# Seven products of quarters for eight in the FFN of a routed-attention kernel

## The chip, the cores and the metric

The kernel runs on one core of a Trainium2 chip. The metric is the device time of one execution in microseconds (us); a time of the kernel is the median of several runs. A profile shows one execution: its span goes from the first to the last recorded instruction, and its own time is a little longer than the span.

## The reference

Two blocks in float32. The first is attention with pooled queries: 8 batches, 8 heads, 1,152 keys of 64 dimensions; two neighbouring queries are averaged, which leaves 576 query rows.

```python
q_pool = q.reshape(B, H, S // 2, 2, D).mean(axis=3)
scores = scale * np.matmul(q_pool, k.transpose(0, 1, 3, 2))
attn = np.exp(scores - max); attn = attn / (attn.sum(axis=-1, keepdims=True) + 1e-9)
x = np.matmul(attn, v)                  # joined over the heads: (8, 576, 512)
```

The second picks, in each batch, the 128 tokens with the highest gate score, and adds a gated feed-forward network (FFN) to them alone; the other tokens pass unchanged.

```python
scores = np.einsum('bsd,d->bs', x, w_gate)
top = np.argpartition(-scores[b], 128)[:128]
h = np.maximum(x[b, top] @ w1, 0.0)     # 512 -> 1024
out[b, top] = x[b, top] + sigmoid(scores[b, top])[:, None] * (h @ w2)   # 1024 -> 512
```

## The kernel before, in words

The work goes pair by pair: a pair is two heads of one batch, 4 pairs a batch, 32 in all. A pair's 576 queries are done in two halves of 288, so the main loop in `run` has 64 halves, plus one turn at the end. The order of all instructions is written out by hand; each engine works through its own queue in that order, and semaphores hold an instruction until what it reads or overwrites is ready.

One turn h of the loop emits, among other things, the following.

- On odd h, the DMAs on SP's queue: `load_pair` (keys `kb`, queries `qb`) two pairs ahead, `load_values` (`v_sb`), and `stored`, which writes a finished pair's `x` to the output (L964).
- `scores` (L807): 36 matmuls on PE in 9 groups. Each group takes one of four PSUM tiles from `banks` (two banks each), and ACT turns it into exponents `p` (L825). PE may run four tiles ahead of ACT.
- `folded` (L850): POOL adds thirds of `p` into `acc` (L857, three instructions), DVE reduces `p` and `acc` into `fold` (L862), which gives the sums of the softmax.
- `multiplied` (L919): POOL makes `prod` from the half two turns earlier and the gate weights; `gated` (L973): DVE reduces it into `red`.
- On even h, `prepare_pair` (L726): POOL adds neighbouring queries (`qp`), and DVE transposes `kT` and `qT` for the pair whose scores begin two turns later.
- `weighted` (L827): 36 matmuls on PE for the half before, then ACT's copy `two` (L844) and POOL's add `av` (L846); `drained`: DVE's transpose `avb` (L915).
- On odd h, `normalized` (L932): DVE's reciprocal `rec`, POOL's product `x` (L956).
- `units`: each batch that is being routed is moved on by one step, newest batch first.

`routed` (L997) is the route of one batch, a generator that is cut into steps by `yield`. A step ends at a `yield` of something true. The steps of a batch, one a turn, begin when its last pair is done: gate scores gathered (`groups`, `line`, `total`) and sent through DRAM to a row `sc_row`; ranks by comparison, on DVE, with two or three of five tiles a step (L1082, L1091, L1101); ranks sent through DRAM (`row_rank`, `lines`); the chosen tokens found on DVE (`pick`, L1161), POOL's `index` (L1170) and the gather of the 128 rows by an indirect DMA on POOL's queue (`xe`, L1178); PE's transposes into `xeT` (L1192); layer 1 (L1203, 32 matmuls of 128 columns in two PSUM tiles, and ACT's Relu, L1211); layer 2 (L1216, 8 matmuls of 512 columns), ACT's product with the gate (`y`, L1235), POOL's add to `xe` (L1238) and an indirect DMA that writes the rows back (L1239). So a batch has one turn with a burst of layer 1 and the next with a burst of layer 2.

The last three batches differ. Layer 2 of batch 5 is held back until after the loop. There, `run` (L1371 on) interleaves by hand the rest of batch 5 (`older`), the FFN of batch 6 (`old`) and the whole route of batch 7 (`new`): `diag` (L1043), its broadcast by matmul (L1053), columns (L679), ranks, `meta` (L1147), the gather, the FFN. Work of `older` and `old` fills PE while `new` waits.

`tile_pool`s give the buffers: a name in a pool has `bufs` slots, and a new tile of that name waits until the readers of the slot's last tile are done.

## Time and profile before

| | before |
|---|---|
| median of 3 runs | 707.98 us (707.88 to 709.09) |
| the profiled execution's own time | 707.99 us |
| its span | 706.3 us |
| mean granted TensorE clock | 0.999 |
| PE, weight load, DVE, ACT, POOL busy | 695.8, 499.9, 494.4, 442.8, 484.9 us |
| L1203 (layer 1), PE busy | 59.3 us in all |
| L1216 (layer 2), PE busy | 57.3 us in all |
| data moved by DMA | 82.86 MB, mean 117 GB/s |

Engines are named PE (matmul), PEld (weight load), DVE, ACT, POOL and SP, and L1203 is a line of the kernel. A group's row has its busy time, the mean length of one instruction, and the idle time of the engine ahead of it with what ended it. The chain that ended last is followed back from the last instruction, at each step to what released it. Each float32 matmul is recorded as two instructions, so counts of PE are twice those of the code.

### The profile page before, as it was taken

What the parts mean: (1) busy time and instruction counts of PE and PEld (TensorE: products, weight loads), DVE (VectorE), ACT (ScalarE), POOL (GpSimd) and SP (SyncE); (2) the same over time, 40 slices, a digit from 0 to 9 for tenths busy, and PEclk for the clock granted to TensorE, in tenths of its full rate; (3) what the DMA queues carried; (4) which work ended last, traced back from release to release, by engine and by line L of the source; (5) the groups of instructions that cost most, each with busy time, mean ns of one, the idle gap of its engine ahead of it and who ended that gap; (6) DMA issues with size and microseconds to landing.
All of it is one profiled execution on the core that took longest, in us unless ns stands there. A gap on an engine that the chain in (4) does not pass through costs nothing.

```text
span 706.3 us, 23391 instructions
## 1 busy us (share of the span) xinstructions
PE 695.8 (99%) x9948; PEld 499.9 (71%) x9948; DVE 494.4 (70%) x793; ACT 442.8 (63%) x963; POOL 484.9 (69%) x452
## 2 busy tenths in 40 slices
PE   8999999999999999999999999999999999999996
PEld 5668889977857678577775777767776677767573
DVE  3877777896549965499654987549784597869540
ACT  6677777777547774477745777467754777577210
POOL 5877777877668685586955879557884777866520
PEclk9999999999999999999999999999999999999999
DMA  9888887849692296825867258652877428442200
GB/s 181 172 170 181 182 166 139 151 95 164 116 169 57 66 165 126 154 52 106 166 104 135 52 126 159 119 106 52 163 127 134 86 53 172 72 82 60 47 31 35
DMA packets 389490, 82.86 MB, mean 117 GB/s; under 512 B 376640, under 2 KB 376640, under 8 KB 389376
## 3 DMA queue, kind: packets, MB, share of 16 engines
q1 hardware_dynamic: 387872, 76.49, 57.4%
q0 software_dynamic: 1280, 4.20, 1.7%
q8 instruction: 80, 1.31, 0.8%
q10 hardware_dynamic: 224, 0.59, 0.3%
q14 instruction: 34, 0.28, 0.1%
HBM read 69.65 MB, written 11.59 MB: 115 GB/s over the span
## 4 chain that ended last, share of the span: by engine, by line
PE 92%; POOL 3%; issue 1%; DVE 1%; DMA 1%; ACT 1%; SPq 0%; POOLq 0%; DVEq 0%; ACTq 0%
PE ps L818 38%; PE ps L836 37%; PE ps L1203 8%; PE ps L1216 7%; POOL acc L857 2%; DMA kb<-in_k_dram 1%; PE ps L1192 1%; POOL prod L925 0%; ACT p L825 0%; POOL x L956 0%; DVE fold L862 0%; POOL av L846 0%; SPq L759 0%; PE ps L1147 0%; PE ps L1053 0%
## 5 line engine op out<-in xcount | busy, mean ns | idle before, releaser
L825 ACT ACTIVATE p<-ps 128x576 f32<-128x576 f32 x576 | 319.2, 691 | 2.6 <-PE ps L818 2.3
L857 POOL TENSOR_TENSOR acc<-p 128x576 f32<-128x576 f32 x192 | 266.1, 1413 | 50.4 <-ACT p L825 50.0
L818 PE MATMUL ps<-qT,kT 64*64 64x288 f32 x4608 | 296.0, 405 | 0.3 <-ACT p L825 0.3
L836 PE MATMUL ps<-p,v_sb 64*64 64x288 f32 x4608 | 294.1, 403 | 0.0
L836 PEld LDWEIGHTS ps<-p,v_sb 64*64 64x64 f32 x4608 | 213.2, 133 | 67.8 <-ACT p L825 14.3
L818 PEld LDWEIGHTS ps<-qT,kT 64*64 64x64 f32 x4608 | 193.3, 132 | 89.8 <-ACT p L825 18.5
L862 DVE TRANSPOSE_TENSOR_REDUCE fold<-p 128x54 f32<-128x1728 f32 x64 | 126.0, 1969 | 117.2 <-ACT p L825 117.2
L862 DVE TRANSPOSE_TENSOR_REDUCE fold<-acc 128x54 f32<-128x1728 f32 x64 | 124.8, 1951 | 42.0 <-POOL acc L857 41.9
L844 ACT COPY two<-ps 128x576 f32<-128x576 f32 x64 | 40.9, 638 | 126.1 <-PE ps L836 113.2
L846 POOL TENSOR_TENSOR av<-two 128x288 f32<-128x288 f32 x64 | 51.1, 798 | 28.9 <-ACT two L844 27.3
L956 POOL TENSOR_TENSOR x<-avb,rec 128x576 f32<-128x576 f32 x32 | 37.0, 1157 | 43.1 <-DVE rec L954 27.1
L1203 PEld LDWEIGHTS ps<-xeT,w 128*128 128x128 f32 x512 | 57.8, 192 | 2.7 <-issue 2.6
L1203 PE MATMUL ps<-xeT,w 128*128 128x128 f32 x512 | 59.3, 277 | 0.0
L1216 PE MATMUL ps<-w,hT 128*128 128x512 f32 x128 | 57.3, 598 | 0.0
L925 POOL TENSOR_TENSOR prod<-avb,w_gate 128x288 f32<-128x288 f32 x64 | 51.3, 802 | 0.6 <-DVE avb L915 0.6
L902 ACT ACTIVATE sums<-total,tiny 32x18 f32<-32x18 f32 x124 | 38.2, 308 | 13.1 <-DVE total L893 11.4
L732 POOL TENSOR_TENSOR qp<-qb 128x576 f32<-128x576 f32 x31 | 43.8, 1412 | 2.5 <-DMA qb<-in_q_dram 2.5
L1216 PEld LDWEIGHTS ps<-w,hT 128*128 128x128 f32 x128 | 23.6, 190 | 28.1 <-issue 28.0
L735 DVE STREAM_TRANSPOSE kT<-kb 128x1152 f32<-128x1152 f32 x31 | 42.5, 1369 | 0.0
L1211 ACT ACTIVATE hT<-ps 128x512 f32<-128x512 f32 x16 | 9.6, 597 | 47.7 <-PE ps L1203 47.7
L1238 POOL TENSOR_TENSOR xe<-y,xe 128x512 f32<-128x512 f32 x7 | 8.9, 1270 | 38.3 <-ACT y L1235 38.3
L915 DVE STREAM_TRANSPOSE avb<-av 128x288 f32<-128x288 f32 x64 | 29.2, 456 | 7.2 <-POOL av L846 7.2
(95 smaller groups left out, 326.1 us busy)
## 6 DMA issues: line engine op xcount, KB each, us to landing
kb<-in_k_dram SPq DMA_DIRECT2D x124, 144.0 KB, 3.6
qb<-in_q_dram SPq DMA_DIRECT2D x124, 144.0 KB, 3.9
v_sb<-in_v_dram SPq DMA_DIRECT2D x124, 144.0 KB, 3.4
out_dram<-x SPq DMA_DIRECT2D x128, 72.0 KB, 3.0
lines<-row_rank SPq DMA_DIRECT2D x7, 640.0 KB, 4.1
w<-in_moe_w_dram SPq DMA_DIRECT2D x8, 512.0 KB, 4.8
sc_row<-row SPq DMA_DIRECT2D x7, 288.0 KB, 3.4
acc<-in_q_dram ACTq DMA_DIRECT2D x2, 288.0 KB, 4.2
```

The costliest lines, as they stand in the source:

```text
L732: nc.gpsimd.tensor_tensor(out=qp[:, :, :], in0=pair["q"][:, :, 0, :], in1=pair["q"][:, :, 1, :], op=ALU.add)
L735: nc.vector.transpose(kT.rearrange("p (c g i) -> p c g i", c=self.NC, i=BLK), pair["k"].rearrange("p (g c) d -> p c g d", c=self.NC),)
L818: nc.tensor.matmul(sc[keys, j, 0:n], lhsT=pair["kT"][rows, c * P + keys.start : c * P + keys.stop], rhs=pair["qT"][rows, qs], start=True, ...
L825: nc.scalar.activation(p[:, c // G, c % G, :, :], sc[:, :, 0:n], AF.Exp, scale=self.scale)
L836: nc.tensor.matmul(av[j * self.D : (j + 1) * self.D, e, 0:n], lhsT=half["pair"]["v"][keys, j, c, :], rhs=half["p"][keys, c // G, c % G, j, :],
L844: nc.scalar.copy(two[:, :, :], av[:, :, 0:n])
L846: nc.gpsimd.tensor_tensor(out=half["av"][:, :], in0=two[:, 0, :], in1=two[:, 1, :], op=ALU.add)
L857: nc.gpsimd.tensor_tensor(out=acc[:, u, :], in0=units[:, 0, u, :], in1=units[:, 1, u, :], op=ALU.add)
L862: nc.vector.tensor_reduce(fold[:, a, :], of.rearrange("p u (m d) -> p (u m) d", d=BLK), AX.X, ALU.add, apply_transpose=True,)
L925: self.nc.gpsimd.tensor_tensor(out=pair["prod"][:, ns, :], in0=pair["avb"][:, ns, :], in1=self.w_gate[:, hp : hp + 1, :].broadcast_to([P, ...
L1203: nc.tensor.matmul(pv[:, f, 0:w], lhsT=self.w1[:, c, (f0 + f) * P : (f0 + f + 1) * P], rhs=xeT[:, c, 0:w], start=(c == 0), stop=(c == self ...
L1216: nc.tensor.matmul(ps[0:w, 0 : self.Dm], lhsT=hT[:, f, 0:w], rhs=self.w2[:, f, :], start=(f == 0), stop=(f == self.NFC - 1),)
```

## The change

The FFNs of batches 0 and 1, 2 and 3, 4 and 5 are done together. The two batches' 2 x 128 tokens form one matrix, cut into quarters (a batch by half of the inner dimension), and the weights are cut into quarters as well. Each layer is then the product of two 2 x 2 block matrices, formed with seven block products in place of eight (Winograd's form). It needs four sums of input quarters (`input_sums`, on POOL), four sums of weight quarters (`weight_sums`, on DVE) and seven additions of products (`add`, on DVE, out of PSUM; the first product is copied by ACT).

- The weight sums of both layers are formed once, at the head of odd turns from h = 11 on, and kept in DRAM. One tile `tw` (128 x 4 x 1024) holds those of one layer; `load_sums` brings them back in four DMAs of 512 KB on SP's queue, a piece a turn.
- An even batch of the six stops after its transposes. The odd one goes on for both: input sums; a turn later layer 1 in one burst, and Relu, now from SBUF over 1,024 columns for each batch; a turn later the input sums of the hidden layer; four turns of loads; layer 2 in one burst; then, a turn each, add and write-back of the two batches; then four turns of loads.
- For batches 4 and 5, the held back step is layer 2 of both.
- Batches 6 and 7 keep the old form, which moves into a function `layers`.
- Buffers: `kb`, `qb`, `two`, `prod`, `sc_row` have one slot in place of two, `v_sb` two in place of three, `fold` and `groups` two in place of four; several scratch tiles share the slot of `pick`, and `diag` that of `lines`; `xe`, `index`, `own_gate` get more slots. The first pair is loaded into a `p` tile. V values are loaded one pair ahead rather than two, behind the keys and queries of the pair after.
- In the tail the pieces are counted anew.

In the built program, each two batches have 56 matmuls of 128 columns and 28 of 256 where there were 64 of 128 and 16 of 512.

```diff
+    def weight_sums(self):
+        for layer in (2, 1):
+            b11, b12, b21, b22 = (self.quarter(layer, i, j) for i in range(2) for j in range(2))
+            t1, t2, t3, t4 = (self.summed(layer, i) for i in range(4))
...
+            for i, (to, x, y) in enumerate(((t1, b12, b11), (t2, b22, t1), (t3, b22, b12), (t4, b21, t2))):
+                nc.vector.tensor_tensor(out=to, in0=x, in1=y, op=ALU.subtract)
+                nc.sync.dma_start(kept[:, i, :], self.tw[:, i, :])
+                yield
+
+    def load_sums(self, layer):
+        for i in range(4):
+            self.nc.sync.dma_start(self.tw[:, i, :], self.tw_kept[layer][:, i, :])
+            yield
...
-        kb = self.load.tile([P, self.KB, BLK], F32, name="kb")
-        qb = self.load.tile([P, self.QB, 2, BLK], F32, name="qb")
+        kb = self.load.tile([P, self.KB, BLK], F32, name="kb", bufs=1)
+        qb = self.load.tile([P, self.QB, 2, BLK], F32, name="qb", bufs=1)
...
-        v_sb = pair["v"] = self.load.tile([P, 2, self.NC, self.D], F32, name="v_sb", bufs=3)
+        v_sb = pair["v"] = self.load.tile([P, 2, self.NC, self.D], F32, name="v_sb", bufs=2)
...
-        two = self.small.tile([P, 2, n], F32, name="two", bufs=2)
+        two = self.small.tile([P, 2, n], F32, name="two", bufs=1)
...
+            if b >= self.paired:
+                yield from self.layers(token)
+            elif b % 2 == 0:
+                self.first_of_two = token
             else:
+                yield from self.layers_of_two([self.first_of_two, token])
...
+    def input_sums(self, a11, a12, a21, a22):
...
+        for to, x, y, op in (
+            (s1, a21, a22, ALU.add),
+            (s2, s1, a11, ALU.subtract),
+            (s3, a11, a21, ALU.subtract),
+            (s4, a12, s2, ALU.subtract),
+        ):
+            self.nc.gpsimd.tensor_tensor(out=to, in0=x, in1=y, op=op)
...
+    def seven_products(self, layer, a, s, c, shape):
...
+        tile = self.banks()
+        nc.scalar.copy(c11, product(bank(tile, 0), a11, b11))
+        yield False
+        add(u, product(bank(tile, 1), s2, t2), c11)
+        yield False
+        tile = self.banks()
+        p5 = product(bank(tile, 0), s1, t1)
+        add(c12, p5, u)
+        yield False
+        add(c21, product(bank(tile, 1), s3, t3), u)
+        add(c22, p5, c21)
+        yield False
+        tile = self.banks()
+        add(c11, product(bank(tile, 0), a12, b21), c11)
+        yield False
+        add(c12, product(bank(tile, 1), s4, b22), c12)
+        yield False
+        tile = self.banks()
+        add(c21, product(bank(tile, 0), a22, t4), c21)
+
+    def layers_of_two(self, tokens):
...
+        s = self.input_sums(*a)
+        yield True
...
+        yield from self.seven_products(
+            1, a, s, c, lambda bank: bank.rearrange("p (f n) -> p f n", n=P)[:, :, 0:w]
+        )
+        for tile in hidden:
+            nc.scalar.activation(tile[:, :, 0:w], tile[:, :, 0:w], AF.Relu)
+        yield True
+        s = self.input_sums(*c)
+        for i, _ in enumerate(self.load_sums(2)):
+            yield "hidden" if i == 3 else True
...
+        yield from self.seven_products(
+            2, c, s, [y[0:w, i * half : (i + 1) * half] for y in ys for i in range(2)],
+            lambda bank: bank[0:w, 0:half],
+        )
+        for token, y in zip(tokens, ys):
+            nc.scalar.activation(y[0:w, :], y[0:w, :], AF.Copy, scale=token["gate"][0:w, 0:1])
+        yield True
+        for token, y in zip(tokens, ys):
+            xe = token["xe"]
+            nc.gpsimd.tensor_tensor(out=xe[0:w, :], in0=y[0:w, :], in1=xe[0:w, :], op=ALU.add)
+            self.written(token)
+            yield True
+        if tokens[1]["b"] + 1 < self.paired:
+            for _ in self.load_sums(1):
+                yield True
...
                     if n + 2 < len(pairs):
                         loaded = self.load_pair(*pairs[n + 2])
-                        self.load_values(loaded)
+                    if n + 1 < len(pairs):
+                        self.load_values(upcoming)
...
+                if h > 10 and s == 1:
+                    next(sums, None)
...
-        pieces(older, self.NFC - 2)
+        pieces(older, 3)
         pieces(new, 1)
-        pieces(older, 2)
+        pieces(older, 1)
         pieces(new, 3)
         pieces(older)
-        pieces(old, self.NFC)
+        pieces(old, self.NFC // 2 - 1)
         pieces(new, 1)
         low = self.counted()
-        pieces(old, self.NFC - 3)
+        pieces(old, self.NFC // 2 + 1)
         pieces(new, 2)
         pieces(old)
```

## The prediction

> **What bounds the kernel.** I read the page's busy shares first, then the chain that ended last, in order of time, then each engine's timeline around one FFN and over the last 100 us.

> The first view is parts 1 and 4 of the page:

> ```profile
> PE 695.8 (99%) x9948; PEld 499.9 (71%) x9948; DVE 494.4 (70%) x793; ACT 442.8 (63%) x963; POOL 484.9 (69%) x452
> ...
> PE 92%; POOL 3%; issue 1%; DVE 1%; DMA 1%; ACT 1%; SPq 0%; POOLq 0%; DVEq 0%; ACTq 0%
> ```

> PE is never idle for long and is 92% of the chain; every microsecond of matmul taken out is won, unless another engine then comes last. The 3% of POOL is the place to watch. The chain in order of time around one FFN (start, length, what):

> ```profile
> 181.89 7.34 PE ps L1203 x64
> 189.23 4.53 PE ps L818 x72
> 193.76 4.37 PE ps L836 x72
> 198.12 7.06 PE ps L1216 x16
> 205.19 4.53 PE ps L818 x72
> ```

> A half (scores, then weighted) is 4.37 + 4.37 = 8.74 us where no FFN stands; each fp32 matmul is recorded as two passes. Layer 1 is 32 matmuls in 7.34 us (0.229 each), layer 2 is 8 in 7.06 us (0.883 each). The scores behind each burst take 4.53, so a burst costs 0.16 more. The same view of the tail:

> ```profile
> 640.39 1.16 POOL x L956
> 641.55 0.08 issue
> 641.63 0.23 POOL gate L1113
> 641.87 4.10 POOL acc L857 x3
> 645.97 0.76 POOL prod L925
> 646.73 0.76 POOL av L846
> 647.49 2.37 issue
> 649.90 0.93 POOL index L1170
> 650.83 0.27 issue
> 651.10 1.11 POOL xe L1178
> 652.25 2.66 POOL acc L857 x2
> ```

> Here, in the last halves, it is POOL's queue that runs end to end and leads to L1043's diag at 664.90; PE has no slack over it.

> **Removed: matmuls.** The built program has, per two batches, 56 matmuls of 128 columns and 28 of 256, for 64 of 128 and 16 of 512. Layer 1: 56 x 0.229 = 12.85 for 14.68. For 256 columns, the line through 114.7 ns (128) and 441 ns (512) a pass gives 223.6 ns, 0.447 a matmul: 28 x 0.447 = 12.52 for 14.12. Bounds for that product: 0.442 (half of 0.883) to 0.459 (twice 0.229), 0.4 us in all. Three pairs: 5.5 + 4.8 = **-10.3**. The 11 bursts in the loop, 0.16 each, go too: **-1.8**.

> **Added on POOL: the input sums.** Each pair gets four adds of 256 columns and four of 512. Rows: prod, 288 columns, 0.80; xe<-y,xe, 512 columns, 1.27. So 2.8 and 4.9 us per pair, 23 us over the run. In the sum this is nothing as such (POOL is 69% busy); it counts where POOL is the chain.

> In the tail it is. The sums of batches 4 and 5's hidden layer stand, in the built order, behind gate L1113 and ahead of the next half's acc, just where the lines above have 641.87. In the trace x ends there 5.2 us behind the half's start at 636.35; behind a burst, as it will stand after, it ends 3.5 behind (217.6 for the half at 214.09 in POOL's timeline). 4.9 - 1.7 = 3.2. The gather of batch 6 (651.10) is then later by that, and PE, which in the trace already waits 0.62 us for it at L1192, waits on. **+3.3**, between 0 (POOL catches up) and 4.9.

> **Added on DVE and ACT: the joins.** Seven DVE adds a layer, out of PSUM, 512 and 256 columns, and one ACT copy. The trace has adds of 384 columns at 0.554 and 576 at 0.758: 0.69 and 0.42, back to back some 0.62 and 0.36. ACT's Relu now comes after them, over 1,024 columns (about 1.0 us from L1211's 0.60 for 512), ahead of the next half's exponents in ACT's queue; behind those wait all scores. The trace prices such a late start: after the transposes at 171.86, the exponents start 1.41 us behind the scores and PE loses 0.70; after L1203 they start 0.80 behind and it loses 0.16. So PE loses the delay less 0.70.
> - Layer 1, first two pairs: POOL ends x 5.0 us into the half before (186.9 for 181.89), the sums at 7.9, acc 4.15 later, 3.4 into the half; then on DVE fold, 1.95, and sum, kT, qT, avb and total, another 3.3: the adds start about 8.7 us into the burst, keep up from the fifth product on and end 0.75 behind it, Relu 1.0 more: delay 1.75, loss 1.05 each, 2.1.
> - Third pair: the ranks of batch 6 (631.48 to 635.7 in DVE's timeline, about 3 us) stand ahead of the adds. They start near 11.7, end 3.2 behind the burst, exponents 4.15 behind: 3.45.
> - Layer 2 in the loop, two pairs: POOL's 4.9 us in the half behind layer 1 carries on, since DVE is full with ranks there (fold waits only 0.84 us for acc at 240.97). About 4.4 us are left when the picks are due. In the trace the rec behind a gather ends 256.2, 7.1 behind the end of weighted at 249.07; with 4.4 more the adds start 11.5 us into a 12.5 us burst and end 1.5 behind it, y 0.8 more: delay 2.3, loss 1.6 each, 3.2.
> Together **+8.75**. Bounds: 0.16 a burst if both engines are there in time (0.8), 14 if each burst waits as the third does, less the overlap of the layer 2 adds.

> The eight weight sums are one DVE add of 1,024 columns each at the head of odd halves; nearest rows are 0.758 (576 columns) and 1.37 (kT, 1,152). Steady halves have 1.5 to 2.5 us of DVE idle that hide it, but where ranks stand it does not: in the half of the transposes qT is ready at 265.9, 2.0 us ahead of the scores that need it (267.86), and two sums ahead of it make 2.5 less what POOL's waits absorb. Half a microsecond at each of the two batches of the first pair: **+1.0**, 0 to 3. [...]

> **Tail: two scatters, then a gather.** The rows on POOL and the landings over the tail's DMA view:

> ```profile
> 672.12 1.09 POOL L1239 DMA_INDIRECT out_dram<-xe,index  x1 [0.29 <-POOL xe L1238]
> 678.35 1.05 POOL L1178 DMA_INDIRECT xe<-out_dram,index  x1 [5.14 <-ACT own_gate L1155]
> ...
> out_dram<-xe,index POOLq DMA_INDIRECT x3, 2.9
> xe<-out_dram,index POOLq DMA_INDIRECT x1, 3.3
> ```

> Before, batch 5's write was long landed when batch 7's index came. After, layer 2 of batches 4 and 5 ends in the tail; its last three adds stand on DVE behind batch 7's ranks and pick (676.4 in the trace, about 676.9 after). From there: adds and y to 678.4, xe add 1.27, write of batch 4 at 680.0, landed 682.9; write of batch 5, which by the built program's semaphores waits for that landing, 683.0 to 685.9; the gather waits for the second landing, 686.0 + 3.3, so PE has batch 7's tokens at 689.4. PE meanwhile has 5.4 us of older's products, 2.75 of layer 1 of batch 6, 1.33 of meta and 4.59 of layer 1, and is out of work at 683.3. **+6.0**; 5.8 with the shortest landings seen (2.8), 8.1 with the medians over the run (3.4 and 4.4), 3 as a floor, if ranks and adds end 3 us sooner than their rows say.
> [...]

> **Hidden.** 28 more DMAs of 512 KB, on SP: the DMA view shows 4.8 us to land for such a piece of w, and the 16 engines are 60% busy. K and Q tiles are single now: the load waits for kT's read (243.25 to 244.6), then some 7 us of issue and 4 of landing, and the next kT read is 17.5 later. V is loaded behind it, needed 17 us after. Each costs nothing while 4 us of that are left. One buffer for two: its reader av is done at 243.84, the next write is due at 249.19, so 5.35 us of cover for POOL's lag of 4.9; gone, ACT's exponents wait, by the price above. prod's single tile is written at 240.91, 3.4 us behind the read it must await; fold, groups, sc_row and the tiles now shared with pick are reused in orders that already hold on DVE. The first pair's V values come behind the second load now: about 33 for a reader at 35.4.

> **Sum.** -10.3 - 1.8 + 3.3 + 8.75 + 1.0 + 6.0 = +6.95. Layer 2 of batch 4 moves from the loop to the tail; PE is full in both, so the move itself costs nothing, and its saving is in the 10.3. The profiled execution took 707.99 (span 706.3 and 1.7 around it), the median of the runs is 707.98. Forecast **715.0**.

> **Rivals.**
> - **The queues keep up (faster).** POOL and DVE work off the sums inside the bursts: adds reached before 8 us into each burst, batch 6's gather on time. Then the losses are 0.8 for the bursts, 0 for the sums, 6.0 in the tail: -12.1 + 6.8 = 702.7. For: both are at 70%, and L862 waits 117 us in total for ACT. Against: those waits lie in halves without ranks.
> - **Single buffers decide (slower).** If 11 us from kT's read to landed Q become over 17.5 because 28 pieces and the lines broadcasts share the engines, every pair stalls. For: the first ten slices show 80 to 90% DMA. At 0.4 us over 25 pairs, 10 on top: 725.
> - **Not done as said.** The built order has exactly 7 products a layer; with eight, the joins would leave 725. Next to nothing.

> **Chances.** Forecast and its neighbourhood (709.5 to 721) 0.60; queues keep up 0.15; a mix within 0.2% of before, about what a measurement here can tell from no change, 0.08; single buffers or worse 0.17. Faster 0.15, same 0.08, slower 0.77. Adding all low ends gives 700, all high ends 726; the range 704 to 722 leaves out half of the first rival and most of the last.

> **What would show it.** Right: two groups of matmuls at 12.85 and 12.5 us; scores behind the third layer 1 burst near 8 us; PE waiting about 4 us and 6 us at the last two transposes, for DMA; POOL and DVE near 73% each. Wrong: scores behind the bursts at 4.5, no wait of PE for a gather, or K loads as what ends PE's idle time.

## The result and the profile after

The changed kernel takes 780.75 us (median of 4 runs, 778.46 to 786.32) where the kernel before takes 707.94: a ratio of 1.104, 95% interval 1.098 to 1.110. Forecast were 715.0 in a range of 704 to 722. The sign was right, the size not: +73 us for +7.

The profiled execution took 781.66 us with a span of 779.9, 73.6 more than before. PE's busy time and idle time split that: busy 695.8 to 710.7 (+14.9), idle 10.5 to 69.2 (+58.7), though the change takes some 10 us of matmuls out. Parts 1 and 4 of the page after:

```profile
PE 710.7 (91%) x9972; PEld 543.9 (70%) x9972; DVE 530.8 (68%) x843; ACT 444.5 (57%) x963; POOL 511.4 (66%) x476
...
PE 58%; POOL 18%; issue 10%; DVE 6%; DMA 4%; ACT 3%; SPq 1%; POOLq 0%; DVEq 0%; ACTq 0%
```

No engine became the bound; PE's share of the chain fell from 92% to 58%, and what came in is waiting on others. (DVE and POOL at 68 and 66% of a longer span are lower than the 73% that the prediction wanted to see.) Where PE waits is read off its timeline. Here is the first burst of layer 1, start, length, what, and in brackets the idle time ahead with what ended it:

```profile
271.63 2.05 PE L1332 MATMUL ps<-xeT,w 128*128 128x128 f32 x16
274.45 3.81 PE L1332 MATMUL ps<-s,tw 128*128 128x128 f32 x32 [0.77 <-ACT hT L1344]
281.54 3.35 PE L1332 MATMUL ps<-s,tw 128*128 128x128 f32 x16 [3.28 <-DVE hT L1338]
284.68 2.30 PE L1332 MATMUL ps<-xeT,w 128*128 128x128 f32 x16
287.85 2.02 PE L1332 MATMUL ps<-s,w 128*128 128x128 f32 x16 [0.88 <-DVE hT L1338]
```

A product is 16 recorded matmuls. Products 2, 4 and 6 wait, 1, 3, 5 and 7 do not. The even ones go to the second bank of a PSUM tile whose first bank holds the odd product, and in the built program their first matmul waits on the engine that reads the odd one: ACT's copy for product 2, DVE's adds for 4 and 6. So PE does not run through a burst with the joins behind it; it stops in the middle until the joins have caught up. DVE's timeline at the same place shows why they are late:

```profile
275.08 1.98 DVE L895 TRANSPOSE_TENSOR_REDUCE fold<-acc 128x54 f32<-128x1728 f32 x1 [4.39 <-POOL acc L890]
...
279.93 0.67 DVE L1338 TENSOR_TENSOR y<-ps,hT 128x512 f32<-128x512 f32 x1
280.70 0.69 DVE L1338 TENSOR_TENSOR hT<-ps,y 128x512 f32<-128x512 f32 x1
284.92 0.69 DVE L1338 TENSOR_TENSOR hT<-ps,y 128x512 f32<-128x512 f32 x1 [3.53 <-PE ps L1332]
```

The first join starts 8.3 us into the burst (forecast: 8.7). Product 4, held by the second join, starts when that ends. The six bursts hold 37.5 us of such gaps: 4.9, 4.9 and 6.3 in layer 1, 6.9, 7.1 and 7.4 in layer 2.

The 3.35 us of product 4 is the other half of the story. Its neighbours take 1.9 to 2.0. Stretches of the same trace (length, then busy time and count of PE, PEld, DVE, ACT, POOL, then granted clock, DMA share and GB/s):

```profile
278.17:281.58 3.41, 0.13 (x2) 0.07 (x1) 3.12 (x6) 0.00 (x0) 0.00 (x0) 1.00 0.48 69
281.58:285.00 3.42, 3.42 (x18) 3.42 (x19) 0.08 (x1) 0.00 (x0) 0.00 (x0) 0.56 1.05 165
285.00:288.41 3.41, 2.54 (x21) 2.37 (x21) 2.00 (x3) 0.00 (x0) 0.00 (x0) 0.94 1.06 203
```

After a stretch of 3.41 us in which PE did next to nothing, PE has half its clock for the next 3.41 us. (The record of the granted clock has 0.5 from 281.99 to 285.40; the stretches shown begin 0.41 us ahead of that, hence 0.56 and 0.94.) Ahead of the last 3 us, the record has 37.5 us at 0.5 in the changed kernel, always in multiples of 3.413 us; in the kernel before it has 0.5 only from 705.09 on, the last 1.2 us.

The tail, PE and then POOL's DMA issues:

```profile
706.05 1.09 PE L1225 MATMUL ps<-ident,xe 128*128 128x128 f32 x4 [4.26 <-DMA xe<-out_dram,index]
...
732.38 3.75 PE L1332 MATMUL ps<-w,s 128*128 128x256 f32 x8 [6.90 <-DVE y L1338]
...
749.72 1.08 PE L1225 MATMUL ps<-ident,xe 128*128 128x128 f32 x4 [3.43 <-DMA xe<-out_dram,index]
```

```profile
738.98 1.10 POOL L1289 DMA_INDIRECT out_dram<-xe,index  x1 [0.29 <-POOL xe L1395]
...
742.64 1.02 POOL L1289 DMA_INDIRECT out_dram<-xe,index  x1 [1.25 <-DMA out_dram<-xe,index]
746.21 1.06 POOL L1211 DMA_INDIRECT xe<-out_dram,index  x1 [2.55 <-DMA out_dram<-xe,index]
```

The gather of batch 6 costs PE 4.26 us (forecast: about 4). Write, write and gather do follow each other's landings; but PE's last wait is 3.43 and not 6, because PE itself had lost 6.90 inside layer 2 of batches 4 and 5 just before.

### The profile page after: what moved, and what is told of

It is laid out like the page before. It is cut to its first block, busy times and chain, and to the rows that moved or that the text cites. A ratio compares the mean times of both kernels' runs of the same rounds, so it can differ in the third digit from the quotient of the medians.

```text
span 779.9 us, 23527 instructions
## 1 busy us (share of the span) xinstructions
PE 710.7 (91%) x9972; PEld 543.9 (70%) x9972; DVE 530.8 (68%) x843; ACT 444.5 (57%) x963; POOL 511.4 (66%) x476
## 4 chain that ended last, share of the span: by engine, by line
PE 58%; POOL 18%; issue 10%; DVE 6%; DMA 4%; ACT 3%; SPq 1%; POOLq 0%; DVEq 0%; ACTq 0%
PE ps L869 23%; PE ps L851 23%; POOL acc L890 10%; PE ps L1332 8%; DVE fold L895 3%; POOL s L1309 2%; PE ps L1260 2%; ACT p L858 2%; POOL prod L958 1%; DMA kb<-in_k_dram 1%; PE ps L1247 1%; POOL av L879 1%; DMA xe<-out_dram,index 1%; POOL qp L765 1%; DMA out_dram<-xe,index 1%
## 5 line engine op out<-in xcount | busy, mean ns | idle before, releaser
L851 PE MATMUL ps<-qT,kT 64*64 64x288 f32 x4608 | 304.7, 409 | 10.8 <-ACT two L877 4.9
L869 PE MATMUL ps<-p,v_sb 64*64 64x288 f32 x4608 | 298.3, 406 | 0.0
L851 PEld LDWEIGHTS ps<-qT,kT 64*64 64x64 f32 x4608 | 204.7, 133 | 95.5 <-ACT p L858 35.9
L869 PEld LDWEIGHTS ps<-p,v_sb 64*64 64x64 f32 x4608 | 228.7, 134 | 55.8 <-ACT p L858 15.4
L920 ACT COPY groups<-sum 32x36 f32<-32x36 f32 x124 | 27.3, 220 | 23.2 <-DVE sum L905 21.8
L1379 ACT ACTIVATE hT<-hT 128x1024 f32<-128x1024 f32 x6 | 6.3, 1058 | 50.8 <-DVE hT L1338 50.8
L1391 ACT ACTIVATE y<-y,own_gate 128x512 f32<-128x512 f32 x6 | 4.3, 722 | 51.7 <-DVE y L1338 51.7
L1332 PE MATMUL ps<-s,tw 128*128 128x128 f32 x144 | 20.4, 306 | 13.5 <-issue 7.9
L1332 PE MATMUL ps<-tw,s 128*128 128x256 f32 x72 | 20.3, 440 | 13.2 <-issue 11.1
L1332 PEld LDWEIGHTS ps<-s,tw 128*128 128x128 f32 x144 | 19.3, 218 | 14.5 <-issue 11.7
```

The lines of the kernel that those rows point to most:

```text
L851: nc.tensor.matmul(sc[keys, j, 0:n], lhsT=pair["kT"][rows, c * P + keys.start : c * P + keys.stop], rhs=pair["qT"][rows, qs], start=True, ...
L869: nc.tensor.matmul(av[j * self.D : (j + 1) * self.D, e, 0:n], lhsT=half["pair"]["v"][keys, j, c, :], rhs=half["p"][keys, c // G, c % G, j, :],
L1332: nc.tensor.matmul(args[0], lhsT=args[1], rhs=args[2], start=i == 0, stop=i == n - 1)
```

## The experiments

The theory after reading this: the wait inside a tile, with DVE late, and the clock that follows it (A). Rivals: POOL and DVE late whatever the tiles (B), the rearranged buffers (C). Times are medians; ratios are against runs of the kernel before on the same chip beside them (medians of 707.9 to 709.8), as 95% intervals.

| run | us | ratio | PE idle, us | at half clock, us |
|---|---|---|---|---|
| changed kernel | 780.75 | 1.098 to 1.110 | 69.2 | 37.5 |
| own_tile | 754.27 | 1.059 to 1.064 | 47.9 | 34.1 |
| filled | 786.50 | 1.104 to 1.108 | 57.6 | 41.0 |
| buffers_only | 713.92 | 1.004 to 1.010 | 13.2 | 0 |
| weights_only | 721.21 | 1.014 to 1.024 | 16.4 | 0 |
| pairs_0_3 | 757.78 | 1.064 to 1.068 | 48.6 | 30.7 |
| own_two | 755.28 | 1.061 to 1.065 | 50.2 | 34.1 |
| late_sums | 771.40 | 1.082 to 1.091 | 61.6 | 44.4 |
| late_sums_03 | 754.95 | 1.062 to 1.069 | 45.6 | 30.7 |
| early_two | 761.18 | 1.070 to 1.077 | 54.6 | 27.3 |
| act_queue | 785.21 | 1.103 to 1.110 | 63.7 | 58.0 |
| best_03 | 748.37 | 1.053 to 1.061 | 38.7 | 27.3 |
| no_sums | 728.52 | 1.025 to 1.029 | 30.9 | 13.7 |
| no_loads | 743.82 | 1.045 to 1.051 | 41.3 | 20.5 |
| one_write | 747.79 | 1.048 to 1.056 | 43.6 | 27.3 |
| all_out | 718.47 | 1.012 to 1.019 | 21.7 | 10.2 |
| layer1 | 712.55 | 1.003 to 1.007 | 16.6 | 6.8 |
| layer1_03 | 712.12 | 1.003 to 1.007 | 13.6 | 0 |

(Idle is span less PE busy of the profiled execution; half clock leaves out the stretch in which the core starts and ends. Both are of one execution. It is the longest of its runs for filled, pairs_0_3, own_two, act_queue and layer1, and the shortest for buffers_only, weights_only, late_sums_03 and no_sums.)

### A PSUM tile for each product: own_tile

```diff
-        add(u, product(bank(tile, 1), s2, t2), c11)
+        add(u, product(bank(self.banks(), 0), s2, t2), c11)
```

and the same for products 4 and 6.

> Every one of the seven products gets a PSUM tile of its own; nothing else changes. Theory A (the wait inside a tile): in the changed kernel products 2, 4 and 6 wait until the product in the other bank of their tile has been read, and DVE comes late to read it. With a tile each, product 2 and 4 have nothing to wait for; product 6 takes the slot of product 2 (four slots), whose reader DVE reaches 8.3 us into a layer 1 burst and about 11.5 us into a layer 2 burst, so about 1 and 2.5 us are left: 37.5 us of idle PE inside the bursts become about 10. The granted clock of one half, 37.5 us in all now, should keep only the windows behind the two gathers and one or two others (about 14 us): 10 to 12 us less of slow matmuls. About 780 - 27 - 11 = 742, PE idle about 34 us. Rival B (DVE and POOL are late anyway): what PE no longer waits inside the burst it waits behind it, for the exponents; then 765 to 780, with the idle time moved to the lines of the scores. Rival C (single buffers carry the loss): 775 to 780, and the gaps inside the bursts, once gone, show up nowhere because they were not on the path.

754.27: 26 us won, where A forecast 38; it lies between A's 742 and B's 765. Layer 1's first two bursts run through, here the first (the third keeps 1.37 us ahead of product 6):

```profile
272.37 2.05 PE L1332 MATMUL ps<-xeT,w 128*128 128x128 f32 x16
274.26 5.52 PE L1332 MATMUL ps<-s,tw 128*128 128x128 f32 x48
279.62 1.95 PE L1332 MATMUL ps<-xeT,w 128*128 128x128 f32 x16
```

Layer 2's two bursts in the loop keep one gap each, ahead of product 6, whose slot is that of product 2; here the first:

```profile
344.33 3.41 PE L1332 MATMUL ps<-w,s 128*128 128x256 f32 x8 [3.60 <-DVE u L1338]
```

So the wait inside the tile is shown as a cause, and it is not all: of 37.5 us of gaps in bursts some 9 are left, but others grew (the last gather's from 3.43 to 7.43). The time at half clock hardly fell, because other places took it over, among them one with no long gap:

```profile
251.17:254.58 3.41, 1.31 (x20) 0.33 (x16) 3.34 (x6) 2.67 (x11) 3.03 (x3) 1.00 0.87 188
254.58:258.00 3.42, 3.42 (x36) 1.73 (x40) 1.52 (x2) 3.14 (x6) 3.42 (x4) 0.58 0.27 105
```

Two waits of 0.81 and 1.28 us at the transposes, 2.1 of 3.41 us idle, were enough. This place lies ahead of the first burst, where the two programs are the same: in the changed kernel's trace the waits there are 0.33 and 1.28 us and the clock stays full. So executions differ in such places without any edit.

### The wait filled with matmuls: filled

```diff
+        idle = self.banks()[:, 0, 0:P]
+        for _ in range(14 if layer == 1 else 22):
+            nc.tensor.matmul(idle, lhsT=self.ones[:, :], rhs=self.ones[:, :], start=True, stop=True)
         add(c21, product(bank(tile, 1), s3, t3), u)
```

> Fourteen (layer 1) and 22 (layer 2) extra matmuls of 128 columns with ones stand ahead of product 4, into a tile that nobody reads: they fill the wait of 3.2 to 6.9 us there and add nothing to the outputs. Theory D (idle PE lowers the clock): PE is no longer idle for over 3 us inside the bursts, so the half clock windows behind those waits (about 24 of 37.5 us) go, half of each being lost work: about 780 - 12 = 768, with mean clock about 0.99. Rival E (the clock falls for another reason, load or chance): mean clock stays near 0.974 and the time at 780 or above, up to 790 where the extra matmuls outlast the wait.

786.50, and a mean clock of 0.973 in the profiled execution: both numbers are rival E's. In the places that were filled D is right: no burst in the loop has a half clock stretch any more, where the changed kernel has 17.1 us of them. But the total rose to 41.0 us, since the transposes (1.85 + 1.28 us idle at 174 to 178, a like pair at 253, more at 441) and a wait of 7.0 at 633 now had it. The first two of these stretches, 13.7 us, lie ahead of the first added matmul, so the edit did not make them. The forecast of 768 was wrong: it took the rest of the kernel to stay as it was.

### The parts alone: buffers_only, weights_only, pairs_0_3

```diff
-        self.paired = self.B - 2 - self.B % 2
+        self.paired = 0
```

> All of the rearranged buffers (single kb, qb, two and prod tiles, V two deep and loaded later, fewer of the rest, cmp and tie in one slot) with every batch's FFN as in the kernel before: no pairs, no sums of weights or inputs, the tail's order as before. Theory A: the buffers cost the waits of the scores for the one two tile, 5 to 6 us in the changed kernel but with a POOL that also had 23 us of input sums, and little else: 709 to 715. Rival C (single buffers carry the loss): 730 or more, with K or Q loads ending PE's idle time.

713.92, +0.4 to 1.0%, 3 to 7 us. Rival C does not carry the loss. What the single K tile does is seen on SP's queue, longest waits of the kernel before and of the changed one (us in total, times, longest):

```profile
SPq L1126 <- DVE red L979: 72.7, 7, 16.4
```

```profile
SPq L740 <- DVE kT L768: 144.7, 26, 26.2
```

Before, SP was early everywhere and stood waiting for the ranks (L1126) that it was to write. Now it stands at each K load until DVE has read the last K, and all that is queued behind, the ranks' write and broadcast too, is late: in buffers_only DVE's pick waits 7.0 us in all for the broadcast, before 0.0.

weights_only adds the eight weight sums and their stores to that (`sums = self.weight_sums()`), unused.

> As buffers_only (no pairs), with the eight sums of the weights and their stores to DRAM added, whose results nobody reads. On record is a price of 1.0 us (0 to 3) for them. Right: 715 (buffers_only 713.9 + 1.0). Theory L (1.5 us each on DVE, in halves with ranks, make the scores late): 717 to 725, with gaps ahead of the scores around 171 and 252 us and a half clock window there.

721.21, about 7 us over buffers_only (1.4 to 2.4% over the kernel before, for 0.4 to 1.0%; its profiled execution, at 715.97, is the shortest of its runs). Theory L, by its time and by gaps of 1.05 and 1.28 ahead of the scores at 175 to 177; the half clock that L forecast is not in this trace, but the mean clock falls from 0.998 in the shortest run to 0.989 in the longest (727.02). Of the adds, for which the prediction had an estimate alone (2.5 for two), four take 1.20 to 1.22 us and four 1.56 to 1.81.

pairs_0_3 leaves batches 4 and 5 and the tail as before (`self.paired = self.B - 4`).

> Only batches 0 to 3 are taken two at a time; 4 to 7 and the tail's order are as in the kernel before, and the buffers stay rearranged. Theory A, by the gaps of the changed kernel: the third pair and the tail hold 6.3 and 7.4 us inside bursts, 3.0 before the third burst, 4.3 and 3.4 at the gathers, 24.5 in all, and about 24 of the 37.5 us at half clock, half of it lost work; 3.4 of matmuls come back: 780 - 24.5 - 12 + 3.4 = 747. If instead each pair costs the same (rival F, a cost per pair and nothing particular to the tail): 780 - 73/3 = 756.

757.78, nearer to a loss that is the same for each pair (756) than to the count of gaps (747): this run gives no sign that the third pair and the tail are anything particular.

### What makes DVE late: own_two, late_sums, early_two

own_two has a tile per product and `two` double again (room from `fold` single, which only DVE uses, and from putting `u` in the place of `c22`).

> A PSUM tile for each product, and the tile two double again as in the kernel before (room for it comes from a single fold tile, which DVE alone writes and reads, and from keeping layer 2's u in the place of c22, which is written after u's last use). Theory G (the single two costs PE): with a tile per product alone, PE waited for ACT's copy into two five times, about 5.8 us with the three xeT waits behind them left out, and two half clock windows (10.2 us) followed: 754.3 - 5 - 5 = 744. Rival H (ACT is late there for another reason, two only being the first thing it does): the same gaps stay, named after the exponents or xeT, and the time stays at 751 to 756.

755.28 for 754.27: H by the time, though PE's gaps ahead of the scores are still put down to `two` (2.72 us at 177). ACT's copy `two` is only the first thing that a late ACT does; doubling its tile, with `fold` single for it, won nothing. The later edits stand on this version.

```diff
+        yield True
         s = self.input_sums(*a)
-        yield True
...
-        s = self.input_sums(*c)
         for i, _ in enumerate(self.load_sums(2)):
             yield "hidden" if i == 3 else True
+        yield True
+        s = self.input_sums(*c)
```

> As own_two, and the input sums are issued directly ahead of their burst instead of a half (layer 1) or four halves and a rank (layer 2) earlier, so that they stand behind acc in POOL's queue; layer 2's burst also comes one half later, out of the half in which the next batch's pick and gather stand. Theory I (DVE comes late to the joins because its fold waits for POOL's acc, and acc stands behind the sums or the gather): the fold's waits of 4.0, 4.7 and 3.4 us go, DVE is at the first add before product 4 ends, the gaps of 3.6 us ahead of product 6 of layer 2 go with their half clock windows: own_two less 7 and less 3.5, about 733, with at most 1.5 us of PE waiting for the sums at product 2 of each burst. Rival J (DVE's own work is what is late: ranks, picks and transposes): the gaps stay, own_two's time within 3 us.

771.40, 16 us worse, which neither theory had. The gaps ahead of product 6 went, as I says; in their place PE waits at product 2 for POOL's sums, 2.9 and 8.2 us in the first pair, where I allowed 1.5: in layer 2 POOL reaches the sums at 351.74, 7.4 us after the burst began. late_sums_03, the same for batches 0 to 3 alone:

> As late_sums with batches 0 to 3 alone in pairs and the tail as before: no third burst, no scatters one behind the other ahead of the last gather. Theory A adds up to: late_sums less the 17.8 us of gaps and about 8.5 us of lost work that the version with a tile per product still has from 610 us on, and 3.4 us of matmuls more: about 710, between 704 and 718; at 705.5 or less it beats the kernel before. Rival K (weight sums, joins and loads have a cost that none of the edits touches): 720 or more.

754.95, where 710 was forecast and K said 720 or more, with the same waits for the sums (2.2 and 8.2 us in the first pair).

early_two puts layer 2 a half earlier instead:

> As own_two, and layer 2's burst comes one half earlier (two of the four loads of its weight sums are issued together), out of the half that holds the next batch's picks, index and gather. Theory M (the gaps ahead of product 6 of layer 2, 3.6 and 4.7 us, come from DVE standing at a fold that waits for POOL's acc behind index and gather): both gaps go and most of the 10 us of half clock behind them: 755.3 - 8 - 5 = 742. In that half DVE's joins should start within 2 us of product 2's end. Rival N (POOL and DVE are behind by then in any half): gaps of 2 us or more ahead of product 6 stay, 750 to 756.

761.18: N by its sign, since the gaps ahead of product 6 are 4.1 us each; the time lies above N's 756, with a gap of 5.96 at L1053 (3.96 in own_two) and new waits for V (1.14 and 1.34 us at 400 to 403). So the half clear of picks and gather was no better.

### SP's queue: act_queue, best_03

```diff
-            self.nc.sync.dma_start(self.tw[:, i, :], self.tw_kept[layer][:, i, :])
+            self.nc.scalar.dma_start(self.tw[:, i, :], self.tw_kept[layer][:, i, :])
```

and the stores likewise, a half later.

> As own_two, and the 28 transfers of weight sums (each store one half later) are issued by ACT instead of SP. Theory O (the waits at the transposes come from SP's queue: the write of ranks is issued behind stores and tw, its broadcast lands late, the pick on DVE waits 2 to 4 us for it, then gather, acc, fold, sum and ACT in turn): the pick's waits for the broadcast fall from 3.3, 4.1 and 2.1 us to at most 1.5, the three gaps ahead of the scores from 4.0, 2.2 and 3.6 to under 2 each, and with them a half clock window or two: 744 to 749. Rival P (the broadcast is late because K and Q's single buffers hold SP up, and tw's 0.5 us issues add little): the pick's waits stay within 1 us of what they were, 752 to 757; more if ACT now waits for landings ahead of the exponents.

785.21, 30 us worse. PE now waits for V (3.98, 3.21, 2.11 and 1.93 us), and SP's waits say why: its own DMAs, which store `x` (L1001) and load V (L754), wait until a transfer that ACT issued has landed.

```profile
SPq L1001 <- DMA tw<-tw: 65.9, 15, 7.8
...
SPq L754 <- DMA tw<-tw: 27.8, 4, 12.2
```

In the built program these are waits on the semaphores that DMAs of all queues share. So the edit brought a wait of its own and says nothing on O.

> All of it: a tile per product, two double, tw by ACT, layer 2 a half earlier, pairs for batches 0 to 3 alone with the tail as before. By the sums of the theories above: own_two less 17.9 of gaps and 8.5 of slow matmuls from 610 us on, less 13 (layer 2's gaps and clock), less 8 (SP), and 3.4 of matmuls more: 711, between 704 and 722. 705.5 or less beats the kernel before. If it stays above 725, at least one of the theories is wrong, or their gains do not add.

748.37, for 711: early_two and act_queue had each failed, so that their gains could not add up here.

### Leaving work out: no_sums, no_loads, one_write, all_out

```diff
-        for to, x, y, op in (
...
-            self.nc.gpsimd.tensor_tensor(out=to, in0=x, in1=y, op=op)
-        return s1, s2, s3, s4
+        return a21, a22, a12, a11
```

> As own_two, with the input sums left out: the products with s1 to s4 take quarters of the inputs in their place, so the outputs of batches 0 to 5 are other numbers, and POOL has 23 us less to do. Theory Q (POOL's sums are what makes DVE, ACT and then PE late in the pairs): the fold's waits of 4 to 4.7 us a half behind the sums go, and with them the gaps ahead of product 6, of L1053 and the window each: 740 or less. Rival R (what is late comes from the chain ranks, broadcast, pick, gather, acc, fold, which the sums do not touch): the gaps ahead of product 6 of layer 2 stay at 3 us or more, those at the transposes stay, 750 to 755.

728.52: Q by its time, and by more than it said. Taking 23 us of work from an engine that is busy 66% of the time won 27 us (22 by the base that one_write gives, below). Of Q's signs the gaps ahead of product 6 went; the gap at L1053 did not (4.70 us for 3.96). The wait ahead of DVE's first join in layer 2 of the first pair, own_two and then no_sums (their bursts start at about 333.0 and 330.45):

```profile
342.27 1.98 DVE L895 TRANSPOSE_TENSOR_REDUCE fold<-acc 128x54 f32<-128x1728 f32 x1 [3.39 <-POOL acc L890]
...
345.07 2.01 DVE L1338 TENSOR_TENSOR y<-ps,y 128x256 f32<-128x256 f32 x5
```

```profile
335.87 1.98 DVE L895 TRANSPOSE_TENSOR_REDUCE fold<-acc 128x54 f32<-128x1728 f32 x1 [3.41 <-POOL acc L890]
...
338.66 2.02 DVE L1329 TENSOR_TENSOR y<-ps,y 128x256 f32<-128x256 f32 x5
```

The fold's wait is the same 3.4 us, but all of it comes 4 us sooner against the burst, and product 6 no longer waits. The sums had been done four halves earlier, so the delay came down from half to half without being made good. That DVE's ranks leave no room for it is an argument; no run takes the ranks away.

> As own_two, with the 20 reloads of weight sums from DRAM left out (the products then use what tw holds, layer 1's sums, so the outputs of batches 0 to 5 are other numbers); the eight stores stay. Theory S (tw's transfers delay the broadcast of ranks): the pick's waits of 4.1, 2.1 and 2.5 us for it behind 420 us go, and the gaps of 2.3 at 434 and 4.0 at 615 with a window each: about 745. Rival T (the broadcast is late because SP holds K and Q loads for the single tiles, with the stores of x behind them): the waits stay within 1 us, 752 to 757.

743.82: S, 11 us won (7 by the base below). The pick's waits for the broadcast behind 420 us are gone, and the gap at L1053 falls from 3.96 to 1.15.

> As own_two, with the write of batch 4's routed rows left out (those rows keep the values from before the FFN). The prediction's tail: the write of batch 5 waits for the landing of batch 4's, and the gather of batch 7 for batch 5's. Right: one landing of 2.9 us and its issue of about 0.8 less, the gap ahead of the last transposes 7.5 to about 3.8, the half clock behind it 6.8 to 3.4: 755.3 - 3.7 - 1.7 = 750. If the gather does not wait for two landings in turn, the gap stays at 7.5 and the time at 755.

747.79; the last two gathers' gaps, own_two and one_write:

```profile
685.35 1.08 PE L1225 MATMUL ps<-ident,xe 128*128 128x128 f32 x4 [4.26 <-DMA xe<-out_dram,index]
...
724.30 1.09 PE L1225 MATMUL ps<-ident,xe 128*128 128x128 f32 x4 [7.47 <-DMA xe<-out_dram,index]
```

```profile
680.42 1.00 PE L1225 MATMUL ps<-ident,xe 128*128 128x128 f32 x4 [4.29 <-DMA xe<-out_dram,index]
...
715.85 1.09 PE L1225 MATMUL ps<-ident,xe 128*128 128x128 f32 x4 [5.03 <-DMA xe<-out_dram,index]
```

The chain of two writes and a gather is shown; leaving out one write won 2.4 us of the gap and not 3.7, because POOL's second add (1.28) then stands ahead of the write that is left.

The time fell by 7.5 us, but not all of that is the write's. Up to it the two programs are the same, and yet one_write is 4.9 us ahead at the gather of batch 6 (680.42 for 685.35); only 2.8 us are won behind it. The two ran on different chips; the kernel before took 709.6 and 709.8 us there, so the versions with late engines vary where the kernel before does not. no_sums and no_loads ran on one_write's chip. Set against one_write and these 2.8 us, 750.6, rather than against own_two, they won 22 and 7 us.

> The three takings-out together, on own_two: no input sums, no reloads of weight sums, no write of batch 4 (outputs differ accordingly). If the losses are separate and add: 755.3 - 26.8 - 11.5 - 7.5 = 709.5, and what is then left of the loss against the kernel before with its 12 us saved, about 13 us, is the weight sums, the buffers and the joins. If POOL's sums and the reloads are late in the same chain and only one of them sets the wait (rival U): 715 to 721.

718.47, in U's range: against own_two the three won 46 us singly and 37 together. But against the base of 750.6 they won 22, 7 and 3, 32 in all, and together 32, so it is not shown that they stand in one chain. With none of these costs, and a tile per product, the kernel is still 1.2 to 1.9% over the kernel before.

### What is left of the idea: layer1, layer1_03

Layer 1 alone in pairs: no reloads, small input sums, layer 2 and the tail as before, a tile per product.

```diff
-        for layer in (2, 1):
+        for layer in (1,):
...
+        for m in self.second(tokens[0], hidden[0]):
+            yield "hidden" if m else False
+        yield from self.second(tokens[1], hidden[1])
```

> Only layer 1 of batches 0 to 5 in pairs with seven products, layer 2 per batch as in the kernel before, and the tail's order as before; so four weight sums, none stored or reloaded, input sums of 256 columns alone (8.8 of POOL's 23 us), a tile per product, two and prod double. By the terms: buffers and weight sums 713.9 and 1 to 4 more, matmuls 5.5 less, and POOL's sums, by their share of what taking them out won, 27 x 8.8 / 23 = 10 more if they are late like the others, 0 if the small ones fit: 709 to 722. At 708 or less the smaller half of the change is worth having.

712.55, slower by 0.3 to 0.7%; its trace is the longest of the four runs, so the half clock in it is not typical. With batches 0 to 3 alone and the weight sums earlier:

> As layer1, with batches 0 to 3 alone in pairs and the four weight sums two pairs of heads earlier, before the first ranks. The third burst of layer1 lost 2.9 us of PE and 6.8 us at half clock, 6.3 in all; matmuls give back 1.8; the sums no longer stand where the first picks do (up to 1.3 at the first transposes): 712.6 - 6.3 + 1.8 - 0.5 = 707.6, between 705 and 711; beside 708 of the kernel before, no change that can be told.

712.12 of 11 runs, no better. The trace has no half clock and 13.6 us of idle PE, 3 over the kernel before; but it is the second shortest of the 11 (709.96, mean clock 0.998), and the longest three (714.21 to 714.38) have 0.994 to 0.996. No version beats the kernel before.

## Why the prediction was wrong, step by step

- **Matmuls, -10.3: nearly right.** In no_sums, where no burst is slowed, the rows of the products sum to 78.6 us, where the prediction has 76.1 (3 x 12.85 + 3 x 12.52); by the rows' busy times the saving is 8.9.
- **Joins, +8.75: the step that failed.** The prediction placed DVE well (8.7 us into the burst for a measured 8.3) and then let PE run on, pricing only what came out behind the burst. In effect it took a two-bank tile for two buffers. In the program it is one: the second product waits for the first one's readers. Those gaps are 37.5 us, and own_tile won 26 of the 73 by taking the wait away.
- **The clock: no term of the sum.** Matmul times were taken from a trace that ran at 0.999. In the 37.5 us at half clock PE was busy for about 33 us. Eight recorded matmuls of 256 columns took 3.75 us there and 1.90 behind it (732.38 and 735.95), so by an estimate some 16 us were lost. That is the larger part of why PE's busy time grew while its work shrank. By the sum, 14.9 + 8.9 (the saving by the rows' busy times) - 16 leaves about 8 us. An estimate accounts for them: a recorded matmul of scores lasts some 0.40 us while the next one starts some 0.06 us after it (72 in 4.37 us), so each wait of PE leaves about 0.34 us of record that no other matmul covers, and PE waits 39 times after for 7 before. No run tests this.
- **Input sums on POOL, nothing in the loop and +3.3 in the tail: wrong by far.** The gather of batch 6 came as late as forecast, but the 23 us of sums cost 22 to 27 in all (no_sums), most of it in the loop. "69% busy" hid that POOL's work stands between ACT's exponents and DVE's folds in each half, so that its delay is passed on.
- **Weight sums, +1.0 (0 to 3): about 7** with the stores (weights_only), though that run spreads over 716 to 727.
- **Hidden at nothing: partly wrong.** `two` was right as far as own_two shows it. The single K and Q tiles and the rest cost 3 to 7 us (buffers_only), and the 20 reloads 7 to 11 (no_loads), through SP's queue and the ranks' broadcast. The prediction gave each load 17.5 us to land and asked whether it was late itself; late was what stood behind it.
- **Tail, +6.0: right in kind.** Once PE is on time the gap is 7.4 us (own_tile); in the changed kernel it shows as 3.43, since PE was late too.
- **Rivals.** "Single buffers decide" named the wrong wait and, with 10 us, a seventh of the 66 that the time lies over the forecast. None of the three had PE waiting inside a burst.
- **Readings.** Two lines were misread, neither with weight in the result: of the first ten slices eight show 80 to 90% DMA, not all (one shows 40%), and the ranks of batch 6 take 3.8 us by their rows (631.48 to 635.30), not 3.

Between own_two and one_write the same instructions differ by some 5 us, so the 73 us are not split into exact shares here.

## What to carry to other kernels

When a burst of matmuls gets readers in its middle, look in the built program at which reader each product's first matmul waits for, and price the wait at that product, not at the end of the burst. Before work is given to an engine with 30% of its time free, find out whether that time lies where the work is needed: here layer 2's sums were done four halves ahead of their burst, and still the gap ahead of product 6 went when they were left out (no_sums). And a saving of matmuls on a bound PE can be lost to waits of PE, once to the wait and again to the clock behind it: here some 10 us were taken out, PE's idle time grew by 58.7, and by an estimate 16 went to the clock.
